# Products of zeros on TensorE in the first microseconds of an attention kernel

## The chip, the cores and the metric

The kernel runs on one core of a Trainium2 chip. The metric is device time in microseconds (us): the execution of the whole program, a little longer than the span that a profile shows (874.33 us timed goes with a span of 872.6).

## The reference

One layer normalization feeds two branches over 2048 tokens of width 640. Branch A is attention with 32 heads of width 20; branch B is a chain of small products with two GELUs; the output is `x + s * g`.

```python
xn = _layernorm(x)
qkv = xn @ wqkv                       # split into 32 heads of 20
scores = einsum("bhqd,bhkd->bhqk", q, k) * (20 ** -0.5)
s = einsum("bhqk,bhkd->bhqd", softmax(scores), v) ... @ wo
g = silu(_B_ref(xn, w1, w2, w3, w4))  # gelu(layernorm @ w1), shifts, @ w2, gelu(layernorm @ w3) @ w4
return x + s * g
```

The exponentials dominate: 32 x 2048 x 2048 of them, in 1024 portions of 128 x 1024. 826 portions go to ACT (ScalarE), one instruction of about 1 us each; DVE (VectorE) makes the rest with integer arithmetic. Everything else must keep ACT supplied.

## The kernel before

A planner written in Python puts every instruction into a fixed order on each engine before the program is built; the chip then runs each engine's list with semaphores between them. So the order on each engine is settled before the run.

The start: tokens come in, are normalized on DVE, GpSimd and ACT, and are transposed by PE (TensorE), four small products to a set, one for each group of 32 columns. The copies back are split between ACT and DVE.

```python
self.QM = self.alloc("QM", [2, 4, 512], BF16)
T("pool", 3500, lambda e: e.memset(self.QM[:, :, :, :], 0.0), writes=[A("QM", k) for k in range(2)], name="qm0", due=-40000.0)
# ... (cut)
self.PVB = 7
T("dve", c_dve(512), lambda e: e.memset(self.bank(self.PVB)[:, :], 0.0), writes=[("PV", 0)], name="pv0")
# ... (cut) in ln1_and_transpose, for 4 groups of 4 tiles and 5 blocks of columns:
    for c in range(4):
        ins = e.transpose(pb[32 * c:32 * c + 32, 128 * bi:128 * bi + 128],
                          xn[:, n, kc * 128 + 32 * c: kc * 128 + 32 * c + 32],
                          self.ident[:, :], tile_position=(0, 32 * c))
    # ... (cut) the copy back on ACT for the blocks in TRA, else on DVE
```

After each quad of heads, the row sums are inverted and the inverses are spread over partitions by a trip through memory: a store of 8 KB (`r0`) and a read of it with broadcast (`r1`), both issued by SP (SyncE), whose list is the order of the transfers.

```python
T("sp", C_SP, lambda e: e.dma_start(dr[ob].rearrange("i (a b) -> (i a) b", b=16), RZ[:, ob, :]), reads=[A("RZ", ob)],
  writes=[("dr", ob)], is_dma=True, nbytes=8192, name=f"r0{quad}_{qc}", stream="r0", dlat=-840.0)
T("sp", C_SP, lambda e: e.dma_start(RB[:, :], bass.AP(dr.tensor, dr[ob].offset, ...)),
  reads=[("dr", ob)], writes=[A("RB")], is_dma=True, nbytes=128 * 2048, name=f"r1{quad}_{qc}", stream="r1", dlat=3600.0)
```

Between the first quads, the projected queries of six further heads are stored (`dk0_0`), and then DVE overwrites their buffer `KS` with absolute values. DVE must wait until the store has read the buffer.

```python
T("sp", C_SP, lambda e, dst=dst: e.dma_start(dst[DH * h0:DH * (h0 + nh), :], KS[0:DH * nh, :]), reads=ksa,
  writes=[("dkq", qk, st)], is_dma=True, nbytes=120 * 4096, dlat=1200.0, name=f"dk{qk}_{st}", stream=f"dk{qk}", due=due)
# ... (cut) in query_bound, with Q = KS:
T("dve", c_dve(cfg.S // 2, "4x"),
  lambda e, k=k: e.tensor_scalar(KS[:, 1024 * k:1024 * k + 1024].bitcast(U16), Q[:, 1024 * k:1024 * k + 1024].bitcast(U16), 0x7FFF, None,
                                 op0=ALU.bitwise_and), ...)
```

## Time and profile before

| before | value |
|---|---|
| three timed runs | 874.76, 875.95, 876.19 us; median 875.95 |
| execution that was profiled | 879.71 us timed, 877.9 span: a slow one |
| PE in the first slice of 21.9 us | three tenths busy |
| first exponential starts | 38.43 us |
| array at half speed until | 22.7 us |

The prediction shows the lines for the start. One more line of the same page matters later, from its part on DMA queues (queue and kind: packets, megabytes, share of the time of 16 engines):

```profile
q8 instruction: 125, 2.05, 1.0%
```

The engines' programs are themselves fetched by DMA while the kernel runs, here in 125 packets of 16.4 KB, 2.05 MB together. I take this queue for PE's: its 31820 products and weight loads come to 255 for each packet. In what follows I count 256 to a packet. That is an estimate from the profiles before and after the change: 31820 instructions needed more than 124 packets, so fewer than 256.6 fill one, and the changed kernel's 32156 came in 126, so at least 255.2 do.

### The profile page before, as it was taken

To read this page: it belongs to the slowest core of one execution; us is meant where nothing else is said; L and a number is where in the kernel's file an instruction comes from. 1 tells how busy PE (TensorE), PEld (TensorE's weight loads), DVE (VectorE), ACT (ScalarE), POOL (GpSimd) and SP (SyncE) were. 2 spreads that over 40 slices of the span, in tenths; PEclk is the share of its full clock that TensorE was granted. 3 is DMA by queue.
4 is the path that set the end of the run, shared out by engine and by line. 5 is a ranking of instruction groups with operands and counts; after the bars stand their busy time and mean duration, and the time that the engine had idled before them with its cause. 6 is when DMAs were issued, how large, how long until landed. Compare 5 with 4: busy or idle time off the path is not lost.

```text
span 877.9 us, 34790 instructions
## 1 busy us (share of the span) xinstructions
PE 826.6 (94%) x15910; PEld 372.3 (42%) x15910; DVE 731.9 (83%) x1006; ACT 838.5 (96%) x887; POOL 43.8 (5%) x74
## 2 busy tenths in 40 slices
PE   3899999999999999999999999999998999999996
PEld 2434333333344444443454444344333444443485
DVE  7646789999879998889886499699997778899857
ACT  6699999999999999999899999999999999999994
POOL 7600000000000000000110000000000000000000
PEclk9999999999999999999999999999998899999998
DMA  7001523322130002321332212332221112013232
GB/s 225 17 1 32 133 88 87 82 81 82 60 89 12 26 25 53 99 73 36 72 77 76 59 39 74 78 99 56 54 59 52 44 28 70 24 51 110 85 91 93
DMA packets 86482, 59.04 MB, mean 67 GB/s; under 512 B 53056, under 2 KB 77840, under 8 KB 86336
## 3 DMA queue, kind: packets, MB, share of 16 engines
q1 hardware_dynamic: 86336, 56.82, 23.9%
q8 instruction: 125, 2.05, 1.0%
q14 instruction: 21, 0.17, 0.1%
HBM read 42.10 MB, written 10.63 MB: 60 GB/s over the span
## 4 chain that ended last, share of the span: by engine, by line
ACT 65%; PE 24%; DVE 6%; DMA 3%; SPq 1%; issue 1%
ACT arena L1528 61%; PE psum L786 9%; PE psum L1504 6%; PE psum L1486 2%; ACT arena L1898 2%; PE psum L1351 2%; PE psum L1478 2%; PE psum L1392 2%; DVE arena L1555 1%; DMA arena<-in_A_x_dram 1%; DVE arena L1469 1%; DMA queries<-arena 1%; ACT arena L1914 1%; DMA arena<-recips 1%; DVE arena L1186 1%
## 5 line engine op out<-in xcount | busy, mean ns | idle before, releaser
L1528 ACT ACTIVATE arena<-psum 128x1024 bf16<-128x1024 f32 x826 | 769.7, 1037 | 11.4 <-PE psum L1351 3.1
L786 PE MATMUL psum<-arena 128*32 128x320 bf16 (+1 forms) x5952 | 362.8, 336 | 7.4 <-DVE arena L1188 3.0
L1504 PE MATMUL psum<-arena 128*32 128x512 bf16 x4576 | 348.9, 382 | 7.0 <-ACT arena L1528 5.8
L1555 DVE TENSOR_SCALAR arena<-psum 128x1024 uint16<-128x1024 f32 x196 | 238.4, 1216 | 39.5 <-PE psum L1486 39.0
L1469 DVE TENSOR_SCALAR arena<-arena 128x4096 uint16<-128x4096 uint16 (+1 forms) x228 | 237.8, 1068 | 3.6 <-PE psum L1478 2.5
L786 PEld LDWEIGHTS psum<-arena 128*32 128x32 bf16 x5952 | 149.9, 97 | 141.8 <-issue 28.7
L1351 PE MATMUL psum<-arena 128*22 128x512 bf16 x1592 | 152.3, 381 | 0.8 <-DVE arena L1590 0.6
L1504 PEld LDWEIGHTS psum<-arena 128*32 128x32 bf16 x4576 | 97.7, 95 | 130.0 <-ACT arena L1528 91.9
L1478 PE MATMUL psum<-arena 128*22 128x512 bf16 x1568 | 129.3, 380 | 0.6 <-DVE arena L1469 0.6
L1486 PE MATMUL psum<-arena 32*128 32x512 bf16 x840 | 88.4, 387 | 12.0 <-ACT arena L1528 6.8
L1486 PEld LDWEIGHTS psum<-arena 32*128 32x128 bf16 x840 | 22.4, 91 | 101.4 <-ACT arena L1528 80.3
L1351 PEld LDWEIGHTS psum<-arena 128*22 128x22 bf16 x1592 | 40.4, 92 | 49.3 <-issue 7.3
L1478 PEld LDWEIGHTS psum<-arena 128*22 128x22 bf16 x1568 | 36.8, 92 | 43.4 <-issue 8.6
L1232 DVE CAST arena<-psum 128x512 bf16<-128x512 f32 x40 | 27.3, 685 | 19.6 <-PE psum L786 19.4
L1894 DVE CAST arena<-psum 128x512 bf16<-128x512 f32 x48 | 32.8, 683 | 12.8 <-PE psum L786 11.3
L1909 DVE TENSOR_TENSOR arena<-psum,arena 128x320 bf16<-128x320 f32 x32 | 15.5, 485 | 14.2 <-PE psum L786 13.1
L1678 DVE SCALAR_TENSOR_TENSOR arena<-psum,arena 128x320 bf16<-128x320 f32 x32 | 15.4, 485 | 14.1 <-PE psum L786 14.0
L989 DVE BATCH_NORM_STATS2 arena<-arena 128x6 f32<-128x320 bf16 x52 | 22.9, 479 | 3.1 <-DMA arena<-in_A_x_dram 3.1
L1301 POOL TENSOR_SCALAR arena<-arena 128x176 bf16<-128x176 bf16 x16 | 8.6, 536 | 325.2 <-DVE arena L1293 325.0
L1293 DVE CAST arena<-psum 128x320 bf16<-128x320 f32 x32 | 15.0, 485 | 10.9 <-PE psum L786 10.9
L1095 PE MATMUL psum<-arena 128*32 128x128 bf16 x320 | 9.6, 256 | 14.5 <-POOL arena L1004 11.3
L1590 DVE COPY arena<-psum 128x512 f32<-128x512 f32 x28 | 19.2, 684 | 2.7 <-PE psum L1478 1.7
(116 smaller groups left out, 346.8 us busy)
## 6 DMA issues: line engine op xcount, KB each, us to landing
arena<-in_B_w_dram SPq DMA_DIRECT2D x48, 160.0 KB, 2.7
arena<-recips SPq DMA_DIRECT2D x28, 256.0 KB
arena<-arena SPq DMA_DIRECT2D x124, 32.0 KB, 1.9
arena<-in_B_w_dram SPq DMA_DIRECT2D x4, 960.0 KB, 5.9
arena<-in_A_x_dram SPq DMA_DIRECT2D x8, 320.0 KB, 6.0
arena<-in_A_x_dram SPq DMA_DIRECT2D x16, 160.0 KB, 3.2
out_dram<-arena SPq DMA_DIRECT2D x16, 160.0 KB, 2.2
heads<-arena SPq DMA_DIRECT2D x112, 20.0 KB
```

What stands on the lines that cost most here:

```text
L786: ins = e.matmul(pb[32 * c:32 * c + 32, 0:N], lhsT(k, c), rhs(k, c), start=(k == 0), stop=(stop and k == nk - 1), tile_position=(0, 32 * c))
L989: lambda e, li=li, n=n, hh=hh: e.bn_stats(st[:, li, 6 * hh:6 * hh + 6], xn[:, n, hD * hh:hD * hh + hD]),
L1232: T("dve", c_dve(512), lambda e, h=h, c=c: e.tensor_copy(KS[:, 512 * c:512 * c + 512], self.wbank(h)[:, 0:512]), reads=[wa], writes=[A("KS ...
L1351: ins = e.matmul(pb[32 * i:32 * i + 22, 0:512], VA[:, ql, kts[i // 2], i, :], PT[:, slots[i // 2][0].slot, 512 * (i % 2):512 * (i % 2) + 512],
L1469: T("dve", c_dve(w, "4x"), lambda e, v=v, dst=dst: e.tensor_scalar(dst, U[:, ub, 0:w], 0.5, EXP_B[v], op0=ALU.mult, op1=ALU.add), reads=ha ...
L1478: ins = e.matmul(pb[32 * i:32 * i + 22, 0:512], wv, dst[:, at:at + 512].bitcast(BF16), start=first, stop=final, tile_position=(0, 32 * i))
L1486: return e.matmul(out, self.KT[32 * i:32 * i + 32, b, 128 * kt:128 * kt + 128], self.QT[32 * i:32 * i + 32, b, 512 * qc:512 * qc + 512], s ...
L1504: ins = e.matmul(out[32 * c:32 * c + 32, :], self.KT[:, b, 128 * kt + 32 * c:128 * kt + 32 * c + 32], self.QM[:, gb, 2 * a + jj, :], start ...
L1528: lambda e: e.activation(self.PT[:, hp.slot, :], self.psum[:, 512 * hs.slot:512 * hs.slot + 1024], AF.Exp, scale=cfg.scale),
L1555: ins = e.tensor_scalar(U[:, ub, 1024 * at + 512 * k:1024 * at + 512 * k + w], self.psum[:, 512 * hd.slots[k]:512 * hd.slots[k] + w], a_ex ...
L1590: T("dve", c_dve(512), lambda e: e.tensor_copy(Ob[:, :], self.bank(self.PVB)[:, :]), writes=[("PV", 0), A("Ob")], name=f"ob{quad}_{qc}", c ...
L1894: T("dve", c_dve(512), lambda e, h=h, fc=fc, i=i: e.tensor_copy(GT[:, i, fc, :], self.wbank(h)[:, 0:512]), reads=[wa], writes=at, name=f"g ...
```

## The change

The intent: PE starts cold and runs at half speed through the transposes and projections on which ACT waits (0.422 us a set of projections until 22.7 us, 0.217 after). It idles until 11.30 us anyway, so it may as well multiply zeros from the moment that a zeroed buffer exists, and reach full speed before the real work. 34 sets of four 512-column products go ahead of the transposes, 8 more between the transposes and the first projections. They write into the bank that later collects the sums, which starts from zero, so nothing has to be cleaned up.

```diff
+        self.NPF = [34, 8]
 ...
         T("dve", c_dve(512), lambda e: e.memset(self.bank(self.PVB)[:, :], 0.0), writes=[("PV", 0)], name="pv0")
+        for k in range(cfg.NPF[0]):
+            T("pe", c_pe(4, 512), self.warm, reads=[A("QM", 0), A("QM", 1)], writes=[("PV", 0)], name=f"warm{k}")
 ...
+    def warm(self, e):
+
+        for c in range(4):
+            ins = e.matmul(self.bank(self.PVB)[32 * c:32 * c + 32, 0:512], self.QM[:, 0, 0, 0:32], self.QM[:, 1, 0, 0:512], start=True, stop=True,
+                           tile_position=(0, 32 * c))
+        return ins
 ...  (at the end of ln1_and_transpose)
+        for k in range(cfg.NPF[1]):
+            T("pe", c_pe(4, 512), self.warm, reads=[A("QM", 0), A("QM", 1), A("xnT", 0, 0)], writes=[("PV", 0)], name=f"warmer{k}")
```

## The prediction

> **What bounds the kernel now.** I read the page first, then the chain of waits, then the timeline of the first 40 us.
>
> ```profile
> span 877.9 us, 34790 instructions
> ...
> PE   3899999999999999999999999999998999999996
> ...
> PEclk9999999999999999999999999999998899999998
> ...
> ACT 65%; PE 24%; DVE 6%; DMA 3%; SPq 1%; issue 1%
> ```
>
> The span of the profiled run is 877.9 us (the timed median is 875.95). The chain that ended last runs mostly on ACT (61% of the span is the exponentials of L1528). PE has idle room only in the first slice (21.9 us each): three tenths busy. PEclk reads full in every early slice, so that row doesn't betray a cold array; the spacing of the matmuls does:
>
> ```profile
> 17.60 2.33 PE L786 MATMUL psum<-arena 128*32 128x512 bf16 x20 [0.19 <-ACT arena L1102]
> 19.71 0.75 PE L1095 MATMUL psum<-arena 128*32 128x128 bf16 x20
> 20.24 1.07 PE L786 MATMUL psum<-arena 128*32 128x512 bf16 x8
> 21.09 0.65 PE L1095 MATMUL psum<-arena 128*32 128x128 bf16 x16
> 21.52 1.39 PE L786 MATMUL psum<-arena 128*32 128x512 bf16 x12
> 22.74 0.39 PE L1095 MATMUL psum<-arena 128*32 128x128 bf16 x16
> 22.97 0.82 PE L786 MATMUL psum<-arena 128*32 128x512 bf16 x12
> 23.62 0.39 PE L1095 MATMUL psum<-arena 128*32 128x128 bf16 x16
> ```
>
> Columns: start, length, engine and line, tile, count. Four matmuls that fill the four column groups make one set. Starts give the rate: 20 projections take 19.71 - 17.60 = 2.11 us, so 0.422 us a set; 20 transposes take 20.24 - 19.71 = 0.53, so 0.106 a set. From about 22.7 on, 12 projections take 23.62 - 22.97 = 0.65, so 0.217 a set, and 16 transposes 22.97 - 22.74 = 0.23, so 0.058. The same instructions run at half speed until 22.7 us and at full speed afterwards.
>
> Who waits for that slow PE:
>
> ```profile
> 20.47 0.21 ACT L1021 ACTIVATION_READ_ACCUMULATOR arena<-arena 128x1 f32 x1
> 23.09 0.60 ACT L1102 ACTIVATE arena<-psum 128x512 bf16<-128x512 bf16 x1 [2.40 <-PE psum L1095]
> 23.58 0.73 ACT L1023 ACTIVATE arena<-arena 128x640 bf16<-128x640 bf16 x1
> ...
> 24.30 0.59 ACT L1134 ACTIVATE arena<-psum 128x512 bf16<-128x512 f32 x1
> ```
> ```profile
> 14.60 0.86 PE psum L1095 x24
> ...
> 15.48 2.08 ACT arena L1102 x4
> ...
> 17.60 2.33 PE psum L786 x15
> ...
> 24.94 1.27 PE psum L786 x20
> ...
> 38.45 1.92 ACT arena L1528 x2
> ```
>
> The second fence is the chain of waits: from the transposes at 14.60 through the projections to the first exponential at 38.45. ACT stands idle 2.40 us until 23.09 for the last transposes of the second group of four token tiles; its last LayerNorm square (L1023), the absolute queries (L1134), and by them the second key projection at 24.94, queue behind that wait. From 38.45 on no work depends on an absolute time, so what is won before it should reach the end.
>
> [...]
>
> **The change part by part.** Comparing the built instruction orders: ACT, GpSimd and the DMA queue have the same order as before to the end; PE has the same order plus 168 filler matmuls; DVE has the same instructions, with five positions changed near 24 us, where one statistics step moves ahead of a 0.37 us copy. So there is no reshuffled schedule, and I only have to move times.
>
> 1. *34 filler sets ahead of the transposes.* They wait for the memset of the buffer that they multiply, 3.51 us on GpSimd from 0.80, so they start at about 4.4. Cold they cost 0.427 each, warm 0.217. [...] Before, the first 32 transposes ran at 11.30 and then PE waited 2.26 us for DVE's normalization until 14.60. The first 32 now run warm after the fillers, in 8 x 0.058 = 0.46 us, [...]
> 2. *Transposes at 14.60, warm.* The last input comes from DVE at about 15.0 anyway; the two sets that the first ACT copy needs and its latency shrink by some 0.1 to 0.2. The four ACT copies (2.08 us) stay. Gain about 0.15: the projection of the first keys starts at about 17.4.
> 3. *Six of the eight later filler sets* lie two by two between transposes that wait 0.5 us each for an ACT copy (16.6, 17.1, 17.6). Two warm sets take 0.43, so they fit and keep the array busy. Two more lie before 24.5, where PE waited for ACT anyway. Cost about 0.
> 4. *PE from 17.60 to 22.74, now warm.* That stretch is 10 projection sets and 9 transpose sets: 10 x 0.422 + 9 x 0.106 = 5.17 us (5.14 measured). Warm: 10 x 0.217 + 9 x 0.058 = 2.69. It saves 2.45, but the transposes also wait for three ACT normalizations that run from 17.41 to 19.96, now some 0.15 earlier. Walking it: keys 17.4 to 18.5, transposes to 18.85, two sets to 19.3, transposes to 19.5, three sets to 20.15, last transposes to 20.4. ACT is itself busy to 20.5. The copy that stood at 23.09 can start at about 20.6: 2.5 earlier.
> 5. *On to 38.45.* ACT's square, DVE's small steps and GpSimd's power (25.35, which waited for DVE; GpSimd is held by a memset until 22.98) come about 2.0 to 2.4 earlier; the second key projection at 24.94 follows ACT and comes about 2.3 earlier. From there on PE was already warm, so everything shifts and nothing shrinks further.
>
> Sum: 0.15 + 2.45, less about 0.3 for late fillers and for GpSimd's memset, is a gain of about 2.3 us: first exponential at about 36.1, time 875.95 - 2.3 = 873.6.
>
> **Rivals.**
> - *Products of zeros don't warm the array.* Then the 34 sets run cold, 14.5 us from 4.4 to 18.9; the 64 transposes come after that at 0.106 a set, so the ACT copies start some 5 us late, and the later fillers add about 1: 881 to 882. For it: nothing shows that zeros count. [...] I give it 1 in 10.
> - *The fillers end too late.* [...] The gain can also be lost if the array falls back to half speed in the now half-idle stretch after 17 us; its gaps are below 1 us, so I doubt it. That would make it about 875.5.
> - *Another engine takes over.* DVE, GpSimd's 2.60 us normalization (18.99 to 21.59), or the loads of x become the bound, and the first exponential comes only 1 us earlier: 875. Against: DVE idles 1.77 and 1.26 us for PE in 18 to 23, and GpSimd waits 2.37 for DVE at 25.35.
> - *The gain is swallowed later*, by a stage between 38 and 878 that doesn't move: 876. All engines keep their order, and no DMA waits on a clock, so I see none.
>
> **Range and chances.** Three timed runs spread by 1.4 us[...]. With a gain of 1 to 3.5 in four cases of five the range is 872.3 to 875.2; I widen the upper end a little for the rivals. A step of 2% is 17.5 us, which none of the ways reaches: PE would have to lose all the fillers' time three times over.
>
> **What would show it.** The start of the first exponential: 36.1 if right, 38.4 if nothing was won, 43 if zeros don't warm. [...] The projection of the first keys: 20 matmuls in 1.1 us, not 2.1, starting near 17.4. ACT's idle time before its copy of the second group: gone or below 0.5, not 2.40. The distance from the first exponential to the end: unchanged at 839.5 (877.9 - 38.4) to within 0.5. It is wrong if the fillers stay at 0.427 throughout, if the transposes start after 15.5, or if that distance grows.

The forecast's sum came to a gain of about 2.3 us, to 873.6: 0.15 and 2.45, estimated from the spacings and waits in the trace of before, less an allowance of 0.3. That the fillers are through and the array is warm by 14.60 us is the assumption on which steps 2 to 5 stand. The 0.427 us for a cold set of fillers, from which the first rival's 14.5 us follow, wasn't in the trace of before (0.422); the changed kernel's trace shows it.

## The result, and the profile after

The changed kernel took 875.22, 874.58, 875.77 and 876.52 us (median 875.50), beside 874.76 to 876.25 for the kernel before (median 876.07 of four). The ratio is 0.9997, with a 95% interval of 0.998 to 1.0014. A ratio here is the mean time of one kernel's fast runs over the mean of the other's in the same rounds, so it is not quite the ratio of the medians. A gain of 2.3 us (a ratio of 0.9974) lies outside the interval. All runs together give 875.76 for the changed kernel (12 executions) against 876.18 (67): a difference of 0.4 us with a standard error of 0.3 (from standard deviations of 0.84 and 1.17).

The profiled executions differ by far more, 877.9 to 873.5 us of span. That is misleading: the one of before happened to be a slow run. The page after:

```profile
span 873.5 us, 35127 instructions
...
PE   7899989999999999999999999999998999999996
...
q8 instruction: 126, 2.06, 1.0%
...
ACT 74%; PE 16%; DVE 7%; DMA 2%; issue 1%; SPq 0%
```

PE is now seven tenths busy in the first slice, where it was three tenths. ACT holds 74% of the chain where it held 65%. There are 337 instructions more (168 products with their weight loads make 336), and one more packet of instructions.

The timeline of PE, changed kernel (start, length, engine and line, operation and tile, count, idle before it):

```profile
4.36 9.58 PE L966 MATMUL psum<-arena 128*32 128x512 bf16 x136 [4.36 <-POOL arena L932]
13.77 0.62 PE L1105 MATMUL psum<-arena 128*32 128x128 bf16 x32
14.90 0.76 PE L1105 MATMUL psum<-arena 128*32 128x128 bf16 x32 [0.52 <-DVE arena L1014]
...
17.73 1.26 PE L787 MATMUL psum<-arena 128*32 128x512 bf16 x20
```

The fillers run from 4.36 to about 13.8, and the transposes that waited for DVE before still wait for DVE: the fillers are out of their way. The first keys' projection takes 1.26 us where it took 2.33. The trace's first record of full speed begins at 8.6 us here, and at 9.9 and 7.3 in two further profiles of the same kernel. (The view by stretches prints a granted clock of 1.00 before that first record, so it doesn't show the cold array.) The spacing agrees: the sets of fillers start 0.427 us apart up to 8.6 us and 0.216 apart after it. So zeros do count.

The timeline of ACT, changed kernel, at the place where it had stood idle for 2.40 us:

```profile
20.74 0.60 ACT L1112 ACTIVATE arena<-psum 128x512 bf16<-128x512 bf16 x1
```

The wait is gone. The chain of waits, changed kernel, at the second keys and the first exponentials:

```profile
23.53 1.08 PE psum L787 x20
...
36.90 6.51 ACT arena L1541 x7
```

These stood at 24.94 and 38.45. So the lead that the zeros win is there at the first exponential. It is smaller than predicted, and then something takes it away. Follow the timeline of all engines around 105 us, first of the kernel before, then of the changed one. SPq lines are issues of transfers; the first is the store of the inverses, the second the read behind it:

```profile
105.03 0.34 SPq L1599 DMA_DIRECT2D recips<-arena  x1
...
110.09 0.57 SPq L1601 DMA_DIRECT2D arena<-recips  x1
...
117.17 0.76 DVE L1198 TENSOR_SCALAR arena<-arena 128x1024 uint16<-128x1024 uint16 x2 [1.14 <-DMA queries<-arena]
```
```profile
103.49 0.34 SPq L1612 DMA_DIRECT2D recips<-arena  x1
...
109.15 0.57 SPq L1614 DMA_DIRECT2D arena<-recips  x1
...
116.52 0.76 DVE L1211 TENSOR_SCALAR arena<-arena 128x1024 uint16<-128x1024 uint16 x2 [2.04 <-DMA queries<-arena]
```

The store of the inverses is issued 66.6 us after the first exponential in both, so the lead arrives whole at 103.49 (1.54 us). The read may go only when the store has landed. I call the time from the one issue to the other the round trip: 5.06 us before, 5.66 after. The store of the queries is queued behind that read and lands 6.4 us after its own issue before, 6.7 after, and DVE stands still until it is through: 1.14 us before, 2.04 after. On DVE 0.65 us of the lead are left.

What ACT makes of it, in its own timeline, before and after:

```profile
119.65 1.94 ACT L1528 ACTIVATE arena<-psum 128x1024 bf16<-128x1024 f32 x2 [0.23 <-PE psum L1486]
```
```profile
119.01 1.94 ACT L1541 ACTIVATE arena<-psum 128x1024 bf16<-128x1024 f32 x2 [1.14 <-PE psum L1499]
```

ACT runs out of scores there. To measure this, I take the time from the start of activation 115 to that of activation 130 on ACT (counted from 0, so that the first exponential is activation 31) and call it the stage of the stacked queries. At full pace it takes 14.05 us, as the runs without the wait will show; here it took 15.58 before and 16.49 after.

### The profile page after: what moved, and what is told of

Read it like the earlier page. It is cut to its first block, busy times and chain, and to the rows that moved or that the text cites. A ratio compares the mean times of both kernels' runs of the same rounds, so it can differ in the third digit from the quotient of the medians.

```text
span 873.5 us, 35127 instructions
## 1 busy us (share of the span) xinstructions
PE 830.2 (95%) x16078; PEld 373.4 (43%) x16078; DVE 732.3 (84%) x1006; ACT 837.9 (96%) x887; POOL 43.6 (5%) x74
## 3 DMA queue, kind: packets, MB, share of 16 engines
q1 hardware_dynamic: 86336, 56.82, 23.6%
## 4 chain that ended last, share of the span: by engine, by line
ACT 74%; PE 16%; DVE 7%; DMA 2%; issue 1%; SPq 0%
ACT arena L1541 70%; PE psum L787 6%; PE psum L1517 3%; ACT arena L1911 2%; PE psum L1499 2%; PE psum L1405 2%; PE psum L1364 1%; DVE arena L1568 1%; DVE arena L1482 1%; PE psum L1491 1%; ACT arena L1927 1%; DMA queries<-arena 1%; DMA arena<-in_A_x_dram 1%; DMA recips<-arena 1%; DVE arena L1199 1%
## 5 line engine op out<-in xcount | busy, mean ns | idle before, releaser
L787 PE MATMUL psum<-arena 128*32 128x320 bf16 (+1 forms) x5952 | 358.3, 333 | 6.0 <-DVE arena L1201 3.0
L1691 DVE SCALAR_TENSOR_TENSOR arena<-psum,arena 128x320 bf16<-128x320 f32 x32 | 15.4, 486 | 13.8 <-PE psum L787 13.7
L1922 DVE TENSOR_TENSOR arena<-psum,arena 128x320 bf16<-128x320 f32 x32 | 15.5, 485 | 13.3 <-PE psum L787 12.2
L999 DVE BATCH_NORM_STATS2 arena<-arena 128x6 f32<-128x320 bf16 x52 | 22.9, 480 | 3.3 <-DMA arena<-in_A_x_dram 3.2
L1616 DVE TENSOR_TENSOR arena<-arena 128x512 bf16<-128x512 f32 x28 | 19.1, 683 | 2.1 <-DMA arena<-recips 2.1
```

The costliest lines, as they stand in the source:

```text
L787: ins = e.matmul(pb[32 * c:32 * c + 32, 0:N], lhsT(k, c), rhs(k, c), start=(k == 0), stop=(stop and k == nk - 1), tile_position=(0, 32 * c))
L999: lambda e, li=li, n=n, hh=hh: e.bn_stats(st[:, li, 6 * hh:6 * hh + 6], xn[:, n, hD * hh:hD * hh + hD]),
```

## The experiments

In every table a time is the mean of the fast runs, beside the mean of 11 executions of the kernel before from the same call, on the same chip. All outputs were correct. "Idle" is DVE's idle time just ahead of its overwriting of the queries.

### First round: is there a difference, and which fillers make it

`b_same` and `a_same` are the two kernels unchanged. `early` and `late` keep one half of the change.

```diff
-        self.NPF = [34, 8]
+        self.NPF = [34, 0]     # early
+        self.NPF = [0, 8]      # late
```

> The kernel before, unchanged, run against itself: the size of the noise. The profiled execution of before had its first exponential at 38.43 us and 839.5 us from there to the end; the changed kernel's had 36.88 and 836.6. Theory A (the start gives 1.5 us and the tail of some 838 us varies from execution to execution, [...]with transfers through HBM): ratio 1.000 within 0.002, first exponential again within 0.3 us of 38.4, but the tail differs from 839.5 by over 1 us. Theory B (the tail is a fixed property of each kernel): tail again 839.5 within 0.3.

> The changed kernel again. Both theories: first exponential at 36.9 within 0.3. Theory A: the timed mean is 1.5 us below that of before (ratio 0.998), once enough runs are averaged, and the tail of the profile is again some 838 with a scatter of a us or two. Theory C (the 1.5 us are regularly lost again, in the transfers through HBM at 104 to 117 us, where the profile gave back 0.9 us): ratio 0.9995 or more, and the lead over before again falls from 1.5 to about 0.6 between 102 and 125 us.

> Only the 34 filler sets ahead of the transposes, none of the 8 later ones. If the early ones do the warming and PE's gaps after them are too short to lose it: [...]first keys' projection 1.1 us long, first exponential at 36.9 within 0.3 and time as the changed kernel's. If the 8 later ones are needed to keep the array at speed: projections of 2.1 us again somewhere in 16 to 22 us, first exponential above 37.5.

> Only the 8 later filler sets. The array is cold when they come (16 us on), so each takes 0.43 us, two of them 0.86 between transposes that used to be 0.5 apart: the first keys' projection starts up to 1 us later than 17.6, at half speed. [...] First exponential 38 to 39.5, time equal to before or up to 1 us longer. If they were the useful part, it would be below 37.5.

| run | time | before | ratio (95%) | first exponential | round trip | idle | stage |
|---|---|---|---|---|---|---|---|
| b_same | 876.77 | 876.31 | 1.0006 (0.9993 to 1.0019) | 37.55 | 4.44 | 0.50 | 14.51 |
| a_same | 876.03 | 876.31 | 0.9997 (0.9983 to 1.0010) | 36.77 | 5.93 | 1.65 | 15.66 |
| early | 876.56 | 876.31 | 1.0004 (0.9987 to 1.0020) | 35.70 | 5.50 | 1.52 | 15.53 |
| late | 879.46 | 876.31 | 1.0037 (1.0025 to 1.0049) | 37.09 | 6.37 | 2.40 | 18.03 |

The result stands: no measurable gain. The late fillers alone are harmful, against the expectation of at most 1 us. The first four sets come at half speed (eight products 1.07 us instead of 0.60); the array is at full speed from 18.3 us, earlier than in the kernel before (21.0 to 22.7), and the first exponential comes 0.5 to 1.3 us earlier than there. Yet the run ends 3 us later. So what happens at the start doesn't decide alone. In the stage of the stacked queries PE of `late` runs at half speed once more, for 6.8 us from 120.7 on. The view by stretches (stretch, length, then busy time and count of PE, PEld, DVE, ACT and GpSimd, granted clock, DMA share, GB/s) has it in this line:

```profile
122.00:126.00 4.00, 3.97 (x40) 1.08 (x40) 3.07 (x5) 3.23 (x4) 0.00 (x0) 0.50 0.28 71
```

In the 3.4 us before 120.7 (the length of the half-speed spell of before, 3.41 us from 121.66 on), PE had been busy for 1.39 alone, behind the wait; then the array was at half speed (that the one brings on the other is not shown), and the stage of 14.05 us became 18.03: 2.40 by DVE's wait and 1.6 by the half speed.

### Second round: take the two suspects away

The first suspect is the wait behind the round trip. `b_swap` and `a_swap` exchange, in SP's order and nowhere else, the store of the queries with the read of the inverses just ahead of it, so that the store no longer waits for the round trip. The second suspect is at the start. A DVE step on three elements (one column of ACT's statistics) was slow in the changed kernel. From the timeline of all engines:

```profile
21.61 1.26 POOL L1300 MEMSET arena<- 128x256 bf16 x1
21.69 1.20 DVE L1038 TENSOR_SCALAR arena<-arena 128x3 f32<-128x3 f32 x1
```

It took 1.20 us, where the same step takes 0.16 in the kernel before (at 24.42), and ended with GpSimd's memset, at 22.9; in `early` it took 0.81 and ended with that memset, too, at 22.0. That the memset held it up is a guess from these times. `nolock` moves the two memsets of 1.26 us from GpSimd to DVE and to before the first loads. `best` is both cures on the changed kernel.

```diff
# b_swap, a_swap, best: after the planner has run
+            self.queries_first()
+    def queries_first(self):
+        pl = self.pl
+        order = pl.order["sp"]
+        i = next(k for k, t in enumerate(order) if pl.tasks[t].name == "dk0_0")
+        a, b = pl.tasks[order[i - 1]], pl.tasks[order[i]]
+        order[i - 1], order[i] = order[i], order[i - 1]
+        a.pos, b.pos = b.pos, a.pos
+        a.start, a.finish = b.finish - 1.0, b.finish
# nolock, best (and the same for the column 21:22)
-        T("pool", 1260, lambda e: e.memset(VA[:, :, :, :, 20:21], 1.0), ..., due=None if hf == 0 else self.at(250))
+        T("pool" if hf else "dve", 1260 if hf else c_dve(256), lambda e: e.memset(VA[:, :, :, :, 20:21], 1.0), ..., due=self.at(250) if hf else -39000.0)
```

> The kernel before with two transfers of the DMA queue exchanged near 110 us: the store of the stacked queries no longer stands behind the read of the reciprocals, which waits for a round trip through HBM. In two profiles of before that round trip landed 5.1 and 4.4 us after its issue, with fillers 5.5 to 6.4. If this wait is what makes the stage from 103 to 131 us long or short: VectorE's wait for the queries' store (1.1 us in before) is gone, the stage from exponential 115 to 130 falls from 14.5 to 15.6 us to about 14.4, and the time falls by 0.5 to 1 us (ratio 0.999). If the stage is held by something else (PE's amount of work): unchanged.

> The changed kernel with the same exchange. Theory C (the lead of the start is given back in the wait behind the reciprocals' round trip): the stage from exponential 115 to 130 falls from 15.7 and 16.5 to about 14.4 us, the lead of 1.2 to 1.5 us stays whole behind it, and the time is 1.2 to 1.5 us below that of b_swap and 2 to 2.5 below before (ratio 0.9975). Theory A (scatter alone): about as much below b_swap as the changed kernel is below before, 0.4 us. If the lead is lost elsewhere: stage shorter, time not.

> The changed kernel with the two memsets of the V buffer's extra columns taken from GpSimd (13.4 and 21.6 us, 1.26 us each) and put on VectorE ahead of the first loads, where it idles. In the changed kernel a VectorE step at 21.69 took 1.20 us, ending with GpSimd's memset, where it took 0.16 in before; and two normalizations at 13.35 took 1.85 beside the other memset, not 0.8. [...]the transposes of the first four tiles start about 1 us earlier (13.9, at the end of the fillers), and the first exponential comes at 35.0 to 35.6 in place of 36.8. If they do not disturb each other: 36.8 again. The time follows by at most as much.

> The changed kernel with both: memsets on VectorE, transfers exchanged. If both readings are right the gains add: first exponential near 35.3, stage from exponential 115 to 130 near 14.4, time 3 to 3.5 us below before (ratio 0.9962). If the tail takes back whatever the start gains: ratio 0.9985 or more.

| run | time | before | ratio (95%) | first exponential | round trip | idle | stage |
|---|---|---|---|---|---|---|---|
| b_swap | 875.73 | 876.34 | 0.9994 (0.9974 to 1.0014) | 39.05 | 5.47, hidden | 0 | 14.05 |
| a_swap | 874.37 | 876.34 | 0.9979 (0.9961 to 0.9997) | 36.05 | 5.21, hidden | 0 | 14.05 |
| nolock | 875.52 | 876.34 | 0.9994 (0.9972 to 1.0016) | 35.65 | 6.17 | 2.03 | 16.03 |
| best | 872.70 | 876.34 | 0.9960 (0.9942 to 0.9978) | 35.68 | 6.01, hidden | 0 | 14.06 |

Timeline of all engines, `a_swap`:

```profile
105.78 0.33 SPq L1259 DMA_DIRECT2D queries<-arena  x1
...
107.86 0.58 SPq L1626 DMA_DIRECT2D arena<-recips  x1
...
113.58 0.75 DVE L1223 TENSOR_SCALAR arena<-arena 128x1024 uint16<-128x1024 uint16 x2
```

The store goes first, no idle time stands in the DVE line, and the stage takes 14.05 us. The changed kernel gains 2.0 us on the kernel before, the kernel before only 0.6 with an interval on both sides of 1. Between the two lie 1.4 us, with a standard error of 0.8. So the wait did hold back the lead, as far as these times can tell. `nolock` is the counter-example that completes this: its first exponential is 1.2 us earlier than after's, its round trip is as long as after's, and its time is no better. Its DVE step takes 0.42 us (at 21.76), 0.8 less. (Another memset on GpSimd, of the key buffer, now meets two normalizations at 12.87 us, which take 2.39 together; the second transposes come at 14.97, not at the 13.9 that was expected.) With both cures the start pays most: 872.42 us in the median of `best`.

What this round doesn't tell is why the round trip is longer in the changed kernel, where nothing around 105 us was changed.

### Third round: fewer fillers

If the round trip lengthens because the stage comes earlier against some clock, its length should follow the first exponential. If it follows from the instructions added, it shouldn't. `f24_8` has 24 early sets, `f10_0` has 10; `b_third` and `a_third` are the two kernels unchanged again, with two timed runs each.

```diff
-        self.NPF = [34, 8]
+        self.NPF = [24, 8]     # f24_8
+        self.NPF = [10, 0]     # f10_0
```

> 24 filler sets ahead of the transposes in place of 34, the 8 later ones kept: 32 sets are 128 matmuls with as many weight loads, 256 instructions of PE[...]. In the profiles so far the instruction packets of 16 KB fell at other moments in the kernels with 42 sets, and there the 768 packets of 2 KB that spread the row factors, in the 8 us before the reciprocals' store, took 161 to 178 ns on average, against 130 to 153 without fillers. Theory D (the shifted instruction packets lengthen the broadcast and with it the reciprocals' round trip): here they fall as in before, DMA share of those 8 us is 0.75 to 0.85 as before and not 0.94, round trip 4.4 to 5.5 us, and the time 1.5 us below before. Theory E (the fillers do it by another way, or it is scatter from load to load): share and round trip as the changed kernel's or anywhere. Both: fillers end by about 12 us, first exponential 36 to 37.

> 10 filler sets alone, ended by about 8.7 us and followed by 2.6 us of waiting: too short to warm PE for good, I expect half speed until 17 to 22 us and the first exponential at 37.5 to 38.6. But they shift PE's instruction packets by 80 instructions, as the changed kernel's 336 do (256 + 80). Theory D: DMA share of the 8 us before the reciprocals' store 0.9 or more, round trip 5.2 to 6.4 us, time 0.5 to 1 us ABOVE before. Theory E: as before (0.75 to 0.8; 4.4 to 5.5), time as before.

> The kernel before in another load, for its trace. Theories C and D: DMA share of the 8 us before the reciprocals' store 0.75 to 0.8, round trip 4.4 to 5.5 us, stage from exponential 115 to 130 14.5 to 15.6. If these belong to the load and not to the kernel: anything from 0.75 to 0.96, 4.4 to 6.4.

> The changed kernel in another load, for its trace. Theories C and D: share 0.9 or more, round trip 5.5 to 6.4, stage 15.6 to 16.5 us; first exponential 36.0 to 36.9. If these belong to the load: anything from 0.75 to 0.96, 4.4 to 6.4.

| run | time | before | ratio (95%) | first exponential | round trip | idle | stage |
|---|---|---|---|---|---|---|---|
| f24_8 | 876.27 | 875.97 | 1.0004 (0.9991 to 1.0017) | 38.83 | 5.19 | 1.48 | 15.93 |
| f10_0 | 878.52 | 875.97 | 1.0028 (1.0013 to 1.0043) | 38.17 | 6.23 | 2.47 | 17.81 |
| b_third | 875.66 | 875.97 | 0.9997 (0.9980 to 1.0014) | 38.08 | 4.38 | 0.11 | 14.12 |
| a_third | 875.42 | 875.97 | 0.9994 (0.9977 to 1.0012) | 35.98 | 6.25 | 2.16 | 16.60 |

24 sets were too few to stay warm: they end at 12.2, PE then waits 2.36 us before the second transposes, and the array is at half speed again from 16.4 to 19.8. Ten sets do as little for the real work. From the timeline of PE, `f10_0`:

```profile
14.52 1.04 PE L1105 MATMUL psum<-arena 128*32 128x128 bf16 x32 [2.85 <-DVE arena L1014]
...
17.52 2.33 PE L787 MATMUL psum<-arena 128*32 128x512 bf16 x20 [0.19 <-ACT arena L1112]
```

And from its timeline of all engines, the store, the read and the step on DVE:

```profile
104.78 0.34 SPq L1612 DMA_DIRECT2D recips<-arena  x1
...
111.01 0.57 SPq L1614 DMA_DIRECT2D arena<-recips  x1
...
118.25 0.76 DVE L1211 TENSOR_SCALAR arena<-arena 128x1024 uint16<-128x1024 uint16 x2 [2.47 <-DMA queries<-arena]
```

The array was warm at 8.6 and cold again at 12.0, so the second transposes and the first keys take as long as in the kernel before. That makes `f10_0` the cleanest comparison. Its first exponential, 38.17, is that of the kernel before (38.43, 37.55, 38.08); from there on its four engines and SP have the same instructions in the same order. Yet its round trip is 6.23 us, DVE stands 2.47, and it is 2.55 us slower (6.8 us of half speed in the stage are part of that). The theory of an earlier arrival falls. What is left of the change is that PE's instructions lie 80 places further on in its program: 10 sets of four products and four weight loads.

### Fourth round: move PE's program and nothing else

By the estimate above a packet of the program holds 256 instructions. If what counts is where PE's program is cut into packets, a shift by 80 should hurt, and a shift by 256, a whole packet, should do nothing. The shifts of the runs so far fit: 0 before; 336, which is 256 + 80, after; 64 in `late`; 80 in `f10_0`; 256 in `f24_8`; and 272 in `early`. `b_pad80` and `b_pad256` add 10 and 32 sets of 16 columns, too short to warm anything for long (ten take 0.50 us), to the kernel before. (That the first exponential of `b_pad80` is early goes with an array that happened to be warm from 20.0 on, while in four other profiles of kernels without fillers (the before's, `b_same`, `b_third`, `b_swap`) it turned between 21.0 and 23.6.) `a_pad512` adds 28 to a changed kernel with 28 + 8 sets, for 512 in all. `b_best` is `best` without fillers.

```diff
# b_pad80 (range(32) in b_pad256, range(28) with NPF = [28, 8] in a_pad512)
+        self.NPF = [0, 0]
+        for k in range(10):
+            T("pe", c_pe(4, 16), self.tiny, reads=[A("QM", 0), A("QM", 1)], writes=[("PV", 0)], name=f"pad{k}")
+    def tiny(self, e):     # as warm, with 16 columns instead of 512
# b_best: the kernel before with queries_first() and with the memsets moved as in nolock
```

> The kernel before with 10 tiny sets (16 columns) ahead: 80 instructions more on PE, ended by about 6 us, no warming, every later instruction as before. Theory D (PE's instruction packets shifted by 80 instructions lengthen the reciprocals' round trip): round trip 5.2 to 6.4 us, stage from exponential 115 to 130 over 16 us, time 1 to 3 us above before (ratio 1.001 to 1.0035) with the first exponential as before's (37.5 to 39). Theory E (the place of the packets does not matter): round trip 4.4 to 5.5, stage 14.1 to 15.6, ratio 1.000 within 0.0013.

> The kernel before with 32 tiny sets: 256 instructions, a whole packet. Theory D: as before in everything (round trip 4.4 to 5.5, stage 14.1 to 15.6, ratio 1.000 within 0.0013). Were it the mere number of added instructions: worse than b_pad80.

> 28 tiny and 28 full filler sets ahead and the 8 later ones: 512 instructions, two whole packets, the array busy about as long as in the changed kernel (4.4 to some 14 us). If it warms as the changed kernel does, the first exponential is at 36 to 37. Theory D: round trip 4.4 to 5.5, stage 14.1 to 15.6, so that the lead is kept: time 1.3 to 2 us below before (ratio 0.998). Theory E: as the changed kernel, ratio 0.9995, stage 15.7 to 16.6.

> The kernel best without the fillers (memsets on VectorE, transfers exchanged): the change alone, where the wait that gave its lead back is hidden, is best against this. Theory C: stage 14.05 us in both, first exponential about 37.5 to 38.5 here and 35.7 in best, time 1.5 to 2.5 us above best's 872.7 (mean): 874.2 to 875.2, ratio 0.998 to 0.999. If the fillers are worth nothing even so: 872.7 to 873.

| run | time | before | ratio (95%) | first exponential | round trip | idle | stage |
|---|---|---|---|---|---|---|---|
| b_pad80 | 877.59 | 876.97 | 1.0006 (0.9991 to 1.0021) | 36.85 | 6.33 | 2.43 | 16.44 |
| b_pad256 | 876.44 | 876.97 | 0.9989 (0.9974 to 1.0004) | 37.58 | 4.90 | 0.96 | 14.97 |
| a_pad512 | 875.64 | 876.97 | 0.9984 (0.9969 to 0.9999) | 38.04 | 4.39 | 0.33 | 14.34 |
| b_best | 876.59 | 876.97 | 0.9995 (0.9976 to 1.0014) | 37.65 | 4.93, hidden | 0 | 14.05 |

Timelines of all engines, `b_pad80` and then `b_pad256`:

```profile
103.45 0.34 SPq L1621 DMA_DIRECT2D recips<-arena  x1
...
117.07 0.76 DVE L1220 TENSOR_SCALAR arena<-arena 128x1024 uint16<-128x1024 uint16 x2 [2.43 <-DMA queries<-arena]
```
```profile
104.18 0.34 SPq L1621 DMA_DIRECT2D recips<-arena  x1
...
116.14 0.76 DVE L1220 TENSOR_SCALAR arena<-arena 128x1024 uint16<-128x1024 uint16 x2 [0.96 <-DMA queries<-arena]
```

`b_pad80` issues its store 0.73 us earlier than `b_pad256` and gets past the queries 0.93 us later. A few dozen products of zeros, of 16 columns, were enough for that. Their times differ by 1.2 us, with a standard error of 0.6; against the kernel before, `b_pad80` isn't clearly slower (1.0006, where 1.001 to 1.0035 was expected), so it is the traces that decide here. `a_pad512` restores the short round trip to a kernel with full fillers. It shows another cost of such a shift, too: in the middle of its first keys PE stood for 1.05 us with nothing to wait for in the trace. The first exponential came at 38.04, not at the 36 to 37 expected, and the lead at the start was lost on the spot. I take that stop for a wait for the program itself; no view proves it. It need not be the rule: the profiled execution was the slowest of the six (877.36 us, the others 874.83 to 875.84).

Over all 20 profiles, the nine whose shift is 64 or 80 past a whole packet have a round trip of 5.21 to 6.37 us, and the eleven whose shift is 0 or 16 have 3.98 to 5.52. DVE's idle time (swaps left out) separates without overlap: 1.65 to 2.47 against 0 to 1.52. The border is thin: the longest on the short side are 1.52 and 1.35 with a shift of 16, and 1.48 in `f24_8`.

Idle time and stage go together. In the ten profiles without a swap and without half speed in the stage, it is 14.05 us and the idle time, to within 0.05. One spell of 3.4 us at half speed (`before`, after, `a_third`, `f24_8`) adds 0.4, twice as much (`late`, `f10_0`) 1.6 and 1.3.

`b_best` closes the second round's question: without fillers both cures are worth nothing measurable (0.9995). The fillers under the two cures are worth the ratio 0.9960 against 0.9995, some 3 us, of which 1.97 lie at the first exponential (37.65 to 35.68). These two ratios come from different calls, so the 3 us are uncertain by some 2.

### Fifth round: warm without the shift

`f32_0` has 32 early sets and no late ones, a shift of exactly 256. `early_again` repeats `early`, whose six times had spread from 874.33 to 879.09.

```diff
-        self.NPF = [34, 8]
+        self.NPF = [32, 0]     # f32_0
+        self.NPF = [34, 0]     # early_again
```

> 32 full filler sets ahead and none later: 256 instructions, a whole packet. Fillers end near 13 us, first exponential 35.7 to 37 if the array stays warm as in early. Theory D: round trip 4.4 to 5.5 us, stage from exponential 115 to 130 14.1 to 15.6 us, time 1.2 to 2 us below before (ratio 0.998). Theory E: ratio 0.9995 or more.

> 34 early sets alone (272 instructions, 16 past a packet), in another load. If early's 876.56 us was scatter: mean 874.3 to 875.5 now, first exponential near 36, stage near 15.5. If it belongs to the kernel (the array loses its speed in some executions without the later fillers): again 876 or more with a scatter of 3 us or more, and a lower mean clock in the slower executions.

| run | time | before | ratio (95%) | first exponential | round trip | idle | stage |
|---|---|---|---|---|---|---|---|
| f32_0 | 874.39 | 875.22 | 0.9987 (0.9970 to 1.0004) | 36.54 | 3.98 | 0 | 14.05 |
| early_again | 875.88 | 875.22 | 1.0008 (0.9995 to 1.0020) | 36.12 | 5.52 | 1.35 | 15.36 |

In `f32_0` both parts are as wished: the first exponential is as early as after's, and there is no wait at the queries at all, without any reordering. Its gain of 0.8 us is less than the 1.5 at the start and the 1.2 to 2 expected, and the interval includes zero. `early_again` confirms that 34 early sets alone gain nothing in time. Against the mean of the three profiles of the kernel before, its lead of 1.9 us at the first exponential falls by 0.6 in the stage and by 0.7 between activations 583 and 607. The profiled execution of `early` keeps its lead to the end (a span of 872.6 us against 875.2), but it was the fastest of its six (874.33, mean 876.56): what the others lost is in no trace. This stays open.

## Why the prediction was right or wrong

**The fillers themselves (step 1): right.** They were to start at about 4.4 us, and the steps behind assume that they are through by 14.60; they ran from 4.36 to 13.8. The doubt whether zeros warm the array is settled: full speed from 7.3 to 9.9 us in three profiles.

**The transposes and the stretch to 22.74 (steps 2 to 4): right.** All inputs arrive at a time that varies by up to 1 us between executions, so I count from the second transposes (14.60 before, 14.90 after). ACT's copy of the second group came 8.49 us after them before and 5.84 after: 2.65 us gained, where the prediction has 2.5.

**"On to 38.45" (step 5), and the sum of "about 2.3": a term mis-sized.** From the same mark, the second keys gained 1.71 us (10.34 to 8.63), and the first exponential 1.59 in the mean of three profiles each (23.54 to 21.95). With the inputs' arrival that makes 38.02 to 36.54, a gain of 1.5 and not 2.3. The prediction allowed 0.3 for the late fillers and for GpSimd's memset. It thought only of GpSimd's own work behind the memset. But what came 2.7 us earlier ran into it: DVE's step on three elements (24.42 before, 21.69 after), 1.04 us longer. `nolock`, which takes that memset away, reaches the first exponential 20.68 us after the second transposes, 1.3 sooner than after. The late fillers and the five positions that had changed on DVE cost 0.3 together: `early`, which has neither, needs 21.65.

**"From 38.45 on no work depends on an absolute time, so what is won before it should reach the end": the step that failed.** The rival "the gain is swallowed later" was dismissed with "all engines keep their order, and no DMA waits on a clock, so I see none". The order was indeed kept. But the program is itself data that PE's queue of instructions fetches by DMA, and 336 more instructions move every later fetch against the work. The round trip of the inverses grew with that, from 4.6 to 5.9 us in the mean of three profiles each, and DVE's wait behind it from 0.6 to 2.0 us; the store of the queries, the DVE step, PE and ACT all stand in that line. In three profiles each, the terms are:

| term (mean of three profiles each, us) | before | after | difference |
|---|---|---|---|
| start to first exponential | 38.02 | 36.54 | -1.48 |
| stage of the stacked queries | 14.74 | 16.25 | +1.51 |
| activations 545 to 560 | 15.18 | 14.04 | -1.15 |
| activations 660 to 690 | 40.91 | 40.80 | -0.11 |
| all other activations | 752.33 | 752.61 | +0.29 |
| from the start of the last activation to the end | 14.07 | 13.72 | -0.35 |

The loss is as large as the gain. The third row goes the other way: a second stage of the same kind gains about 1 us from the shift (14.04 to 14.72 us in the profiles with a shift of 64 or 80, 14.76 to 15.88 in the others). The shift is a matter of luck in each place. The sum is -1.28, more than the timed 0.4. The three profiled executions of before were timed 0.85 us above the mean of all its runs, and the three of after within 0.1 of theirs; that accounts for the rest. It also spoils the sign that the prediction named, the distance from the first exponential to the end: 839.5 us before and 836.6 after in the first two profiles, but 837.2 and 837.4 in the mean of three.

That the added instructions and not the earlier arrival lengthen the round trip is shown by `f10_0` (no lead, long trip), `b_pad80` and `b_pad256` (same kernel, shift alone) and `f32_0` (full lead, short trip). That the lead arrives once the wait is hidden is shown by `a_swap` and `best`.

How a fetch lengthens the store's landing is in the records of single DMA packets (kept with the traces; no view of `prof` prints them one by one). The store is 128 packets of 64 bytes. The first of them starts 1.9 to 3.9 us after the issue, for the nine reads ahead of it, which spread the row factors of branch B in 2 KB packets, are still under way. In ten of the eleven profiles with a shift of 16, 64 or 80 the last eight packets then start 0.35 to 1.6 us after the other 120, and a 16 KB packet of program ends in that gap; in none of the nine with no shift does one. (The eleventh is `a_swap`, whose packet of program starts at 67.7 us; its trip is the shortest of the eleven, 5.21.) In `f10_0`, counted from the first exponential, the packet of program runs from 70.00 to 71.56 us, the 120 are under way by 70.40, the eight start at 71.99, and the store lands at 72.82. The gap is of the size of the difference: round trips of 6.0 us in the mean with a shift of 64 or 80, 4.75 with none. Nor is this one place alone: over all 560 such stores of the 20 traces, the last eight lag by more than 0.3 us in 65, and in 56 of these a packet of program ends in the gap; of the other 495, 6 have one there.

Eight of 128 packets is the share of one DMA engine of 16, so I read this as one engine that has program to fetch ahead of its part of the store; which engine carries a packet isn't recorded. Not shown is why the fetch doesn't get ahead of the store with no shift, where a packet of program starts at 69.6 to 70.8 us as well. The share of the DMA engines from 62 to 70 us after the first exponential goes with the shift too, if barely (0.93 to 1.01 in the eight profiles with 80, 0.75 to 0.92 in the twelve others), but within each group it doesn't follow the round trip: `b_third` has 0.92 with 4.38 us, `a_swap` 0.99 with 5.21.

**The range.** Its width was taken from three runs that spread by 1.4 us, but single executions of the kernel before lie between 873.6 and 879.7. Part of that is at one place, for a reason not shown: near 674 us the array falls to half speed for 3.4 us in the profile of after and in `b_same`, but for 10.2 in that of before, and the activations 660 to 690 take 40.33 to 42.07 us in the six profiles of the table.

## What to carry to other kernels

Work without use warmed the array here, and it stayed warm where no long gap came before the real work: 24 early sets with a gap of 2.36 us behind them were too few (`f24_8`), 32 with none above 1.06 us were enough (`f32_0`). A lead is worth only what the next fixed wait lets through, so look for stages downstream where an engine idles on a chain of transfers, and reorder the queue there; here one exchange of two transfers turned nothing into 2 us, and with the memsets moved as well the kernel went from 876.3 to 872.7. And instructions that "cost nothing" still lengthen the program: before believing in a small gain or loss, shift the program by padding and see whether it stays.
